# Sums, products and scalings of an attention kernel moved to GpSimd, its fillers left out, and its order given as tables

## The chip, the cores and the metric

One core of a Trainium2 chip. The kernel is one program for five engines that run side by side and wait for each other through semaphores: TensorE (PE in the profile; PEld is its weight loading), VectorE (DVE), ScalarE (ACT), GpSimd (POOL) and SyncE (SP), which issues nearly all transfers. The metric is the device time of one execution in microseconds; the time before is the median of three runs.

## What is computed

Two attentions over the same input x (2048 rows, 512 columns, 32 heads of 16), mixed by a gate of each row.

```python
def _A_ref(x, wqkv, w_phi, wo):          # linear attention with softmax features
    q, k, v = ...                         # 32 heads of 16
    pq = jnp.einsum("bhsd,hdf->bhsf", q, w_phi)
    pk = jnp.einsum("bhsd,hdf->bhsf", k, w_phi)
    phi_q = jnp.concatenate([_softmax(pq), _softmax(-pq)], axis=-1)
    phi_k = jnp.concatenate([_softmax(pk), _softmax(-pk)], axis=-1)
    kv = jnp.einsum("bhsf,bhsd->bhfd", phi_k, v)
    z  = jnp.einsum("bhsf->bhf", phi_k)
    num = jnp.einsum("bhqf,bhfd->bhqd", phi_q, kv)
    den = jnp.einsum("bhqf,bhf->bhq", phi_q, z)[..., None] + 1e-6
    return (num / den) @ wo               # heads put side by side

def _B_ref(x, wqkv, wo):                 # ordinary softmax attention
    scores = jnp.einsum("bhqd,bhkd->bhqk", q, k) * (Dh ** -0.5)
    return jnp.einsum("bhqk,bhkd->bhqd", _softmax(scores), v) @ wo

g = sigmoid((x * gate_w).sum(-1, keepdims=True))
return g * _A_ref(x, ...) + (1 - g) * _B_ref(x, ...)
```

## The kernel before, in words

**B, the bulk.** Scores are made transposed, keys on partitions and 512 queries along the free axis. There are 2048 such tiles of 128 x 512: 32 blocks (a block is four heads in four row groups of TensorE, with one chunk of 512 queries), 16 key tiles, four heads. A tile's exponential is taken on one of two paths.

- *ScalarE's path*: `add_qk` (L1305) puts two tiles into two PSUM banks, `add_exp` (L1389) takes the exponential of both in one instruction of 128 x 1024 into the ring `Ebuf`, and `add_pv` (L1443) multiplies them with V into the accumulator `psO`. Two pairs of banks alternate, so the scores of pair j + 2 need the exponential of pair j. This makes 652 exponentials.
- *The path of VectorE and GpSimd* (`add_group`, L1360): 744 tiles in groups of up to four. VectorE writes the score, offset and cut at zero, as a 16-bit integer whose bits are read as bf16: an approximate power of two (L1378; L1368 where two neighbouring banks go in one instruction). GpSimd adds a constant to these bits, four 16-bit words at a time, with `int64_add` (`shifted`, L1354), once to get a second term and, after TensorE has used that, once more for a third. `add_pvd` (L1416) multiplies the first two terms with V, and then the third (L1413). Each group holds two buffers from the lists in `PHASES`, which rotate.

The denominator comes as a 17th column of V. `add_norm` (L1504) drains a finished block (L1507), takes the inverse sums through small transfers and a reciprocal (L1516), and VectorE multiplies the result by them (L1523).

**A, beside it.** `phi` (L1658) projects 128 rows at a time onto the features, ScalarE takes both exponentials, and TensorE sums the 16 features of each head with 16 accumulating matmuls against the identity (L1676), two row tiles in one bank. For keys VectorE takes the reciprocal (L1691) and scales V with it (L1650). For queries VectorE takes a reciprocal, a copy and a product (L1682, L1684, L1686), and `scaled_q` (L1699) scales the negative features by the ratio (L1703); transfers then turn the features (`q_write`, `q_turn`). `kfinal` (L1731) masks the product of key features and V (L1732, L1735). `v_pair` (L1165) projects V for two head rows at once, with full 128-column matmuls of 256 (L1166).

**Order.** All work is recorded as operations with an engine, a planned duration, a priority and dependencies. `Plan.layout` (L538) plays the plan through with these durations and so fixes each engine's order and the PSUM banks. It also puts *fillers* on TensorE, matmuls with a zero operand (`zero_mm`, L1401), where its planned activity of the last microseconds falls under a limit. `Plan.settle` (L780) then applies the lists in `MOVES`: instructions of one engine that change places, pairs of VectorE tiles that are joined, banks, and fillers that are dropped. An operation marked `lock` is not planned while the other of VectorE and GpSimd runs one. Each engine runs its list strictly in that order; `emit` (L825) puts a semaphore wait ahead of an instruction where a dependency needs it, and whatever stands behind a waiting instruction on its engine waits too.

Of the kernel before, what the change touches and what calls it, by code (L numbers as in the profile page):

```python
# [9 lines left out]
F32 = mybir.dt.float32  # L10
# [21 lines left out]
PHASES = ((0, ("x0", "x1", "pq", "o3", "y0"), ("y1", "pt", "woA", "woB", "o2")),  # L32
          (16, ("x0", "x1", "n0", "a0", "y0", "wk"), ("y1", "a1", "a2", "a3", "wv")),
          (27, ("x0", "x1", "n0", "a0", "y0", "wk"), ("y1", "a1", "a2", "a3", "wv", "wq")))
SIZES = (2, 2)
STICK = 58.273
# [39 lines left out]
ERING = 2 * EPAIRS  # L76
LAT, BANK_LAT = 0.12, 0.12
# [3 lines left out]
MOVES = {  # L81
# [9 lines left out]
    ),  # L91
    "act": (
# [3 lines left out]
    ),  # L96
# [383 lines left out]
class Plan:  # L480
# [48 lines left out]
    def choose(self, op, banks):  # L529
# [4 lines left out]
        if op.half is not None:  # L534
            self.filled.setdefault(op.half[0], {})[op.half[1]] = (best.index, op.half[1])
# [1402 lines left out]
```

## Time and profile before

| | us |
|---|---|
| runs: median (lowest, highest) | 676.08 (675.73, 676.28) |
| profiled execution, its span | 673.9 |
| TensorE busy | 665.2 (99%) |
| ScalarE busy | 643.0 (95%) |
| VectorE busy | 602.8 (89%) |
| GpSimd busy | 401.0 (59%) |

The profile is of one execution; its span runs from the first to the last recorded instruction. In the lists of groups, a row gives the line, the engine, the operation, output <- input, the shapes and the count, then the busy time of all of them in microseconds and the mean of one in nanoseconds, then the idle time of the engine just before them and what ended most of it. Matmuls overlap each other, so a busy TensorE can still be mostly waiting; the waits tell. In the list of waits, a row gives the waiting engine, tile and line, what it waited for, the total in microseconds, the number of waits and the longest. The row PEclk gives the TensorE clock that was granted, in tenths of the full one, in 40 slices of the span.

### The profile page before, as it was taken

The page shows a single profiled execution, that of the slowest core. Times are in us where ns is not written, and L with a number is a line of the kernel's source. Part 1 is how long each engine was busy: PE and PEld are TensorE (multiplying, and loading weights), DVE is VectorE, ACT ScalarE, POOL GpSimd, SP SyncE. Part 2 cuts the span into 40 slices and gives each one's busy share as a digit, 9 for nine tenths or more (in the row PEclk, how much of TensorE's full clock was granted, in tenths as well). Part 3 has the DMA queues.
Part 4 walks back from the last instruction along what each step waited for, and adds up shares of the span by engine and source line. Part 5 has one row for each costly group of instructions (what it writes and reads, how often), then busy time and mean ns, then how long its engine had stood idle before and what let it go on. Part 6 is the DMA issues. An engine that isn't in the chain of part 4 may idle for free.

```text
span 673.9 us, 20931 instructions
## 1 busy us (share of the span) xinstructions
PE 665.2 (99%) x8995; PEld 233.7 (35%) x8995; DVE 602.8 (89%) x952; ACT 643.0 (95%) x723; POOL 401.0 (59%) x432
## 2 busy tenths in 40 slices
PE   8999999999999999999999999999999999999997
PEld 4332333434333333333333233323333233333333
DVE  4699889999998889999898989899999989999985
ACT  6999999999999999999999999999989998899995
POOL 7055557465666446565577676666865666555862
PEclk9999999999999999999999999999999999999999
DMA  7810101001010000000013032222311224032231
GB/s 129 157 40 12 32 13 26 11 11 23 7 27 11 11 21 8 19 17 15 21 41 102 26 67 62 54 44 64 77 54 41 63 77 105 18 89 66 66 72 40
DMA packets 67468, 30.95 MB, mean 46 GB/s; under 512 B 52696, under 2 KB 62296, under 8 KB 67376
## 3 DMA queue, kind: packets, MB, share of 16 engines
q1 hardware_dynamic: 66368, 28.95, 18.2%
q8 instruction: 70, 1.15, 0.7%
q10 hardware_dynamic: 576, 0.52, 0.2%
q0 software_dynamic: 432, 0.15, 0.2%
q14 instruction: 22, 0.18, 0.1%
HBM read 7.87 MB, written 8.88 MB: 25 GB/s over the span
## 4 chain that ended last, share of the span: by engine, by line
PE 81%; DVE 9%; ACT 7%; DMA 1%; issue 1%; SPq 0%; DVEq 0%
PE psS L1301 29%; PE psO L1413 28%; PE psS L1062 14%; ACT E_t L1392 6%; PE psS L1676 3%; DVE Tx_t L1378 2%; PE psO L1403 2%; DVE Ty_t L1378 1%; PE psS L1153 1%; PE psS L1166 1%; DVE WAT_t L1378 1%; DMA ld<-Tf_t 1%; PE psS L1773 1%; DMA Lq_t<-ld 1%; DVE vA_t L1378 1%
## 5 line engine op out<-in xcount | busy, mean ns | idle before, releaser
L1392 ACT ACTIVATE E_t<-psS 128x1024 bf16<-128x1024 f32 x652 | 611.6, 1049 | 20.0 <-PE psS L1301 16.1
L1301 PE MATMUL psS<-qz_t,kTB_t 32*128 32x512 bf16 x2048 | 272.9, 384 | 3.0 <-ACT E_t L1392 0.8
L1378 DVE TENSOR_SCALAR Tx_t<-psS 128x512 int16<-128x512 f32 x250 | 164.3, 681 | 13.2 <-PE psS L1301 11.8
L1301 PEld LDWEIGHTS psS<-qz_t,kTB_t 32*128 32x128 bf16 x2048 | 72.8, 91 | 231.5 <-ACT E_t L1392 100.7
L1413 PE MATMUL psO<-E_t,vaug_t 128*32 128x512 bf16 (+1 forms) x1304 | 106.4, 383 | 0.1
L1354 POOL INT64_ADD vA_t<-vA_t x72 | 71.5, 1001 | 35.7 <-PE psO L1413 21.3
L1378 DVE TENSOR_SCALAR Ty_t<-psS 128x512 int16<-128x512 f32 x110 | 73.7, 681 | 6.1 <-PE psS L1301 5.5
L1354 POOL INT64_ADD Ty_t<-Ty_t x42 | 43.3, 1032 | 15.0 <-PE psO L1413 10.2
L1413 PE MATMUL psO<-vA_t,vaug_t 128*32 128x512 bf16 (+1 forms) x520 | 49.9, 383 | 0.0
L1378 DVE TENSOR_SCALAR Tz_t<-psS 128x512 int16<-128x512 f32 x62 | 42.0, 685 | 3.3 <-PE psS L1301 2.2
L1413 PE MATMUL psO<-Ty_t,vaug_t 128*32 128x512 bf16 x436 | 43.9, 383 | 0.0
L1378 DVE TENSOR_SCALAR WAT_t<-psS 128x512 int16<-128x512 f32 x58 | 39.2, 685 | 4.2 <-PE psS L1301 3.8
L1354 POOL INT64_ADD phiQT_t<-Tx_t x19 | 18.1, 950 | 40.8 <-DVE Tx_t L1378 37.7
L1378 DVE TENSOR_SCALAR oT_t<-psS 128x512 int16<-128x512 f32 x56 | 37.4, 683 | 5.1 <-PE psS L1301 4.8
L1354 POOL INT64_ADD Ty_t<-Tx_t x29 | 29.7, 1025 | 20.4 <-DVE Tx_t L1378 12.1
L1413 PEld LDWEIGHTS psO<-E_t,vaug_t 128*32 128x32 bf16 (+1 forms) x1304 | 27.4, 95 | 35.3 <-issue 22.5
L1062 PE MATMUL psS<-Wp_t,xT_t 128*32 128x512 bf16 x512 | 37.7, 382 | 0.0
L1378 DVE TENSOR_SCALAR vA_t<-psS 128x512 int16<-128x512 f32 x52 | 35.1, 683 | 2.4 <-PE psS L1301 1.9
L1062 PE MATMUL psS<-xT_t,WB_t 128*32 128x512 bf16 x464 | 36.6, 383 | 0.0
L1354 POOL INT64_ADD vA_t<-Tx_t x22 | 22.0, 1002 | 21.5 <-DVE Tx_t L1378 17.5
L1378 DVE TENSOR_SCALAR Wp_t<-psS 128x512 int16<-128x512 f32 x48 | 31.9, 682 | 2.6 <-PE psS L1301 2.3
L1413 PE MATMUL psO<-Tx_t,vaug_t 128*32 128x512 bf16 x282 | 29.7, 387 | 0.0
(166 smaller groups left out, 914.4 us busy)
## 6 DMA issues: line engine op xcount, KB each, us to landing
dpq<-EA_t SPq DMA_DIRECT2D x16, 256.0 KB, 2.1
Rb_t<-lr SPq DMA_DIRECT2D x120, 32.0 KB, 1.8
dpo<-kv_t SPq DMA_DIRECT2D x16, 128.0 KB, 1.8
qz_t<-qz_t SPq DMA_DIRECT2D x120, 16.0 KB, 1.8
Tf_t<-Tf_t SPq DMA_DIRECT2D x60, 32.0 KB, 2.0
WB_t<-in_B_wqkv_dram SPq DMA_DIRECT2D x3, 384.0 KB, 4.3
out_dram<-WvA_t SPq DMA_DIRECT2D x8, 128.0 KB, 1.9
out_dram<-WB_t SPq DMA_DIRECT2D x6, 128.0 KB, 1.8
```

What stands on the lines that cost most here:

```text
L1062: ins = e.matmul(out[32 * i:32 * i + 32, :], lhsT=lhsT[:, 32 * i:32 * i + 32], rhs=rhs, start=start, stop=stop, tile_position=(0, 32 * i))
L1153: mms = [lambda e, ap, i=i, t=t: e.matmul(ap[:, 128 * i:128 * (i + 1)], lhsT=xT[:, t, NQ * c + 128 * i:NQ * c + 128 * (i + 1)], rhs=W_B[:, ...
L1166: mms = [lambda e, ap, i=i, t=t: e.matmul(ap[:, 256 * i:256 * (i + 1)], lhsT=xT[:, t, NQ * c + 128 * (2 * hf + i):NQ * c + 128 * (2 * hf + ...
L1301: return e.matmul(bank, lhsT=kT_B[32 * i:32 * i + 32, ROW[b // 2] % 2, 128 * kt:128 * (kt + 1)], rhs=qz[32 * i:32 * i + 32, b // 2 % 4, b ...
L1354: op = P.add("pool", P64 + W64 * size, d_prio(g["ts"][0]) - 5.0 + (0.0 if key == "s" else M_LATE), lambda e: e.int64_add(words(dst), words ...
L1378: ops.append(drain(f, mm, "dve", 0.70, d_prio(d), lambda e, ap, q=q: e.tensor_scalar(quarter(tb, q).bitcast(I16), ap, EXPB, 0.0, op0=ALU.a ...
L1392: op = P.add("act", EXP_OVH + 0.4267 * n, 0.0, lambda e: e.activation(Ebuf[:, j // 2 % EPAIRS, 512 * SZ[0] * (j % 2):512 * SZ[0] * (j % 2) ...
L1403: ins = e.matmul((psO if bank is None else bank)[32 * i:32 * i + 32, :], lhsT=zero[:], rhs=xT[:, 0, 0:NQ], start=bank is not None, stop=ba ...
L1413: return e.matmul(psO[32 * i:32 * i + w, :], lhsT=vaug[:, kt, o:o + w], rhs=rhs, start=start, stop=stop, tile_position=(0, 32 * i), skip_g ...
L1676: mms = [lambda e, ap, n=n, f=f: e.matmul(ap[:, 64 * n:64 * n + 64].rearrange("p (s g j) -> p s g j", s=2, j=4), lhsT=ident[:], rhs=es[n][ ...
L1773: mms = [lambda e, ap, g=g: e.matmul(ap[:, 64 * g:64 * g + 64], lhsT=qT(g)[:, 128 * j:128 * (j + 1)], rhs=kzbd[:, g, 0:64], start=True, st ...
```

## The change

- The feature sums of A leave TensorE: GpSimd adds halves four times, 16 features to 8, 4, 2 and 1, as 128 TensorTensor instructions, into the buffers `half` (which lies over the weights `Wbd` and `Wbp`, after their use) and `quart`.
- The product with the inverse sums (15 of them), the ratio of query features (8), the scaling of the negative query features (16) and the two masks of `kfinal` go from VectorE to GpSimd. The copy of the sums is no longer needed. The reciprocals stay on VectorE and read SBUF.
- `v_pair` uses `columns`: four matmuls of 32 columns in place of one of 128.
- No filler is left on TensorE. `layout` and `settle` go; `place` reads each engine's whole order, the banks and the joined pairs from `TABLE`. No operation is locked against another by the plan.
- The buffer `Tz` goes. From the third block on, both halves of `WAT` serve as buffers.
- `WIDE`, a way to give one exponential three tiles, is there but empty.

GpSimd's `int64_add` and its TensorTensor come from different libraries of operations. The build puts an instruction that reloads the library ahead of an operation that the loaded one does not have; copies, casts and fills are in every one. An excerpt of the changed program's order on GpSimd, the number of the instruction ahead (an ISA without operands is a reload; an ISA with tiles is a 64-bit add; L1365 are the sums, L1200 the products):

```
60 L1365 ISA
61 L1365 TensorTensor stat_t<-Wbs_t 128x8x2x4
62 L1029 ISA
63 L1029 ISA WoB_t<-WAT_t 128x1024
...
120 L1365 ISA
121 L1365 TensorTensor Wbs_t<-phiK_t 128x512
122 L1029 ISA
123 L1029 ISA WoB_t<-Ty_t 128x1024
124 L1365 ISA
125 L1365 TensorTensor quart_t<-Wbs_t 128x256
126 L1029 ISA
127 L1029 ISA oT_t<-Tx_t 128x512
```

The diff, cut to its core:

```diff
-PHASES = ((0, ("x0", "x1", "pq", "o3", "y0"), ("y1", "pt", "woA", "woB", "o2")),
+PHASES = ((0, ("x0", "x1", "o3", "y0"), ("y1", "pt", "woA", "woB", "o2")),
+          (2, ("x0", "x1", "n0", "o3", "n1", "y0"), ("y1", "pt", "woA", "woB", "o2")),
...
-MOVES = {
+TABLE = {
...
+    def place(self, table):
+        self.closed = {b: list(b.last) for b in self.every}
+        for b in self.every:
+            b.first = b.free
+        homes = {7 if b.index is None else b.index: b for b in self.every}
+        known, bank = list(self.ops), iter(table["homes"])
+        for k, n in table["extra"]:
+            known[k].extra = n
+        self.order = {e: [known[k] if k >= 0 else self.filler(k) for k in table[e]] for e in ENGINES}
+        for op in self.order["pe"]:
+            if op.acq is not None:
+                op.acq.bank = homes[int(next(bank))]
...
-    Wbd = sb([128, KT, 128], name="Wbd")
-    Wbp = sb([128, KT, 128], name="Wbp")
+    Wbs = sb([128, 2, KT, 128], name="Wbs")
+    Wbd, Wbp = Wbs[:, 0], Wbs[:, 1]
+    half = Wbs[:].rearrange("p a t c -> p (a t c)").bitcast(F32)
...
+    quart = sb([128, 256], F32, name="quart")
...
-        mms = [lambda e, ap, i=i, t=t: e.matmul(
-            ap[:, 256 * i:256 * (i + 1)], lhsT=xT[...],
-            rhs=W_B[:, t, 2 * D + 256:3 * D], start=(t == 0), stop=(t == KT - 1)) for i in range(2) for t in range(KT)]
+        mms = [lambda e, ap, i=i, t=t: columns(
+            e, ap[:, 256 * i:256 * (i + 1)], xT[...],
+            W_B[:, t, 2 * D + 256:3 * D], t == 0, t == KT - 1) for i in range(2) for t in range(KT)]
...
-                P.add("dve", 0.7, -40, lambda e: e.tensor_tensor(oT[:, r, qc, :], Tf[:, 0, :], Rb[:], ALU.mult),
-                      reads=[("Tf", 0), "Rb"], writes=[("oT", qc, r)], name=f"T2.{b}").lock = True
+                P.add("pool", 1.25, -40, lambda e: e.tensor_tensor(oT[:, r, qc, :], Tf[:, 0, :], Rb[:], ALU.mult),
+                      reads=[("Tf", 0), "Rb"], writes=[("oT", qc, r)], name=f"T2.{b}")
...
-        mms = [lambda e, ap, n=n, f=f: e.matmul(ap[:, 64 * n:64 * n + 64]..., lhsT=ident[:],
-                                                rhs=es[n][0]...[:, f],
-                                                start=(f == 0), stop=(f == DH - 1)) for n in range(2) for f in range(DH)]
-        f, mm = fill(S_PRIO + prio, mms, [k for _, k in es] + ["ident"], name=f"S{qk}.{st}", chunk=8, dur=0.042, cols=64)
+        for n, (e_ap, ek) in enumerate(es):
+            src, k = e_ap.rearrange("p (h f j) -> p h f j", f=DH, j=4), DH
+            while k > 1:
+                k //= 2
+                if k > 1:
+                    to = (quart if k == 4 else half)[:, 0:64 * k].rearrange("p (h f j) -> p h f j", f=k, j=4)
+                    u, v = src[:, :, 0:k, :], src[:, :, k:2 * k, :]
+                else:
+                    to = pair[:, n, :].rearrange("p (s g j) -> p g s j", s=2, j=4)
+                    u, v = [src[:, :, x, :].rearrange("p (g s) j -> p g s j", s=2) for x in (0, 1)]
+                P.add("pool", 0.1 + 0.14 * k, prio, lambda e, to=to, u=u, v=v: e.tensor_tensor(to, u, v, ALU.add), ...)
+                src = to
...
-            drain(f, mm, "dve", 0.25, prio, lambda e, ap: e.tensor_copy(statq[...], three(ap)[:, :, 0, :]), ...)
-            P.add("dve", 0.25, prio, lambda e: e.tensor_tensor(ratio[:], ratio[:], statq[...], ALU.mult), ...).lock = True
+            P.add("pool", 0.25, prio, lambda e: e.tensor_tensor(ratio[:], ratio[:], pair[:, :, 0:32], ALU.mult), ...)
...
-        P.add("dve", 0.7, prio, lambda e: e.tensor_tensor(minus, minus, by, ALU.mult), ...).lock = True
+        P.add("pool", 1.25, prio, lambda e: e.tensor_tensor(minus, minus, by, ALU.mult), ...)
...
-        P.add("dve", 2.3, prio, lambda e: e.tensor_tensor(kzbd[:, :, 0:64], kv_sb[:, :, 0:64], mask64[...], ALU.mult), ...).lock = True
+        P.add("pool", 1.3, prio, lambda e: e.tensor_tensor(kzbd[:, :, 0:64], kv_sb[:, :, 0:64], mask64[...], ALU.mult), ...)
...
-    P.layout()
...
-    P.settle(MOVES)
+    P.place(TABLE)
```

More of the change, by code (lines that the diff above doesn't have):

```diff
@@ L35 @@
 SIZES = (2, 2)
+WIDE, WIDE_SPAN = (), (8, 540)
 STICK = 58.273
@@ L76 @@
 ERING = 2 * EPAIRS
+E_AT = [sum(1024 + 512 * (k in WIDE) for k in range(r)) for r in range(ERING + 1)]
 LAT, BANK_LAT = 0.12, 0.12
@@ L523, in join_writes @@
         self.readers[key] = []
-    def mates(self, a, b):
-        return PAIRING and b.kind == "D1" and a.half[0] == b.half[0] and abs(a.rel.bank.index - b.rel.bank.index) == 1 and (
-            a.half[1] - b.half[1]) * (a.rel.bank.index - b.rel.bank.index) > 0
-    def choose(self, op, banks):
-        def key(b):
-            cross = op.half is not None and any((b.index - k) * (op.half[1] - q) < 0 for k, q in self.filled.get(op.half[0], {}).values())
-            return cross, max([0.0] + [x.end for x in b.last])
-        best = min(banks, key=key)
-        if op.half is not None:
-            self.filled.setdefault(op.half[0], {})[op.half[1]] = (best.index, op.half[1])
-        return best
@@ L768, in join, with filler @@
+    def filler(self, kind):
+        op = Op("pe", 0.215, 0.0, None, "idle")
+        op.deps, op.kind = list(self.ground), "zero"
+        if kind == -3:
+            op.acq = op.rel = Fill(self.misc)
+            op.fn = lambda e: self.idle(e, op.acq.bank.ap)
+        else:
+            op.fn = self.idle if kind == -1 else self.idle_o
+        self.ops.append(op)
+        return op
     def join(self, op, other):
@@ L770, in join @@
         b, b2 = op.rel.bank.index, other.rel.bank.index
-        assert other.half[0] == n_g and abs(b - b2) == 1 and (q - q2) * (b - b2) > 0
+        assert other.half[0] == n_g and (q - q2) * (b - b2) > 0
         op.fn = lambda e, a=(min(q, q2), max(q, q2)), b=(min(b, b2), max(b, b2)): wide(e, a, b)
@@ L777, in join @@
         other.rel, other.twin = None, op
-        self.order["dve"].remove(other)
-    def settle(self, moves):
-        homes = {b.index: b for b in self.every}
-        for k, b in moves.get("banks", ()):
-            op = self.order["pe"][k]
-            op.acq.bank, op.banks = homes[b], [homes[b]]
-        q = list(self.order["dve"])
-        for a, k in moves.get("pairs", ()):
-            self.join(q[a], q[k])
-        for a, k in moves.get("locks", ()):
-            self.order["pool"][a].deps.append(q[k])
-        gone = set(moves.get("drop", ()))
-        self.order["pe"] = [o for k, o in enumerate(self.order["pe"]) if k not in gone]
-        for e in ENGINES:
-            q, pairs = self.order[e], moves.get(e, ())
-            left = {a for a, _ in pairs}
-            new = [o for k, o in enumerate(q) if k not in left]
-            for a, k in pairs:
-                new.insert(k, q[a])
-            self.order[e] = new
+    def place(self, table):
[10 more added lines that the diff above has]
+                op.acq.bank = homes[int(next(bank))]
+            op.banks = op.take if op.take is not None else [op.acq.bank] if op.acq is not None else []
+        for a, k in table["pairs"]:
+            self.join(known[a], known[k])
         for op in self.ops:
@@ L1006, in _build @@
                   name="wob", lat=5.0)]
-    warm = P.add("dve", 0.3, -10, lambda e: e.memset(Ebuf[:, 0, 0:512], 0.0), writes=[("E", 0)], name="wz")
+    warm = P.add("dve", 0.3, -10, lambda e: e.memset(Ebuf[:, 0:512], 0.0), writes=[("E", 0)], name="wz")
     def warm_fn(e):
@@ L1229, in _build @@
     cur, rot = 0, 0
+    is_wide = lambda j: j % ERING in WIDE and WIDE_SPAN[0] <= j < WIDE_SPAN[1]
     def next_tile():
@@ L1245, in _build @@
         j = len(slots)
-        act = [t for t in (next_tile() for _ in range(SZ[j % 2])) if t is not None]
+        act = [t for t in (next_tile() for _ in range(SZ[j % 2] + is_wide(j))) if t is not None]
         if not act:
@@ L1271, in _build @@
     bufs["wq"] = (Wp[:, :, 0:D], p_ops[0])
-    for k in range(1):
+    for k in range(2):
         bufs[f"n{k}"] = (flat(WAT[:, 4 * k:4 * k + 4, :]), wp_ops)
@@ L1315, in fn @@
             ins = None
-            for m, t in enumerate(ts):
+            for m, t in enumerate(ts[:2]):
                 ins = qk_mm(e, t, psS[:, 512 * (base + m):512 * (base + m + 1)])
@@ L1320, in add_qk @@
         op.full = 0.21
-        op.kind, op.heads = "qk", [t[1] for t in ts]
+        op.kind, op.heads = "qk", [t[1] for t in ts[:2]]
+        if len(ts) == 3:
+            third[j] = fill(-99, [lambda e, ap: qk_mm(e, ts[2], ap)], reads, [bS[lowS]], name=f"q3.{j}", after=exp_ops[j - 2:j - 1])
+            third[j][1].kind, third[j][1].heads = "q3", [ts[2][1]]
         op.lat += QK_PAD
@@ L1329, in add_qk @@
         return op
-    made, dq_ops, last_d1 = [0], [], []
+    made, dq_ops, last_d1, third = [0], [], [], {}
     holder = {}
@@ L1392, in add_exp @@
         op = P.add("act", EXP_OVH + 0.4267 * n, 0.0, lambda e: e.activation(
-            Ebuf[:, j // 2 % EPAIRS, 512 * SZ[0] * (j % 2):512 * SZ[0] * (j % 2) + 512 * n], psS[:, 512 * base:512 * (base + n)], ACTF.Exp, scale=ESCALE),
-            reads=[("S", j % 2)], writes=[("E", j % ERING)], name=f"exp{j}")
+            Ebuf[:, E_AT[j % ERING]:E_AT[j % ERING] + 512 * n], psS[:, 512 * base:512 * (base + n)], ACTF.Exp, scale=ESCALE),
+            reads=[("S", j % 2)], writes=[("E", j % ERING)], after=[third[j][1]] if j in third else [], name=f"exp{j}")
+        if j in third:
+            op.rel = third[j][0]
         op.kind, op.extra = "exp", j % 2
@@ L1453, in add_pv @@
                 pv_started.add((b, t[1]))
-                o = 512 * SZ[0] * (j % 2) + 512 * m
-                work.append((seen[t[1]], t, Ebuf[:, j // 2 % EPAIRS, o:o + 512], start))
+                o = E_AT[j % ERING] + 512 * m
+                work.append((seen[t[1]], t, Ebuf[:, o:o + 512], start))
                 seen[t[1]] += 1
@@ L1480, in add_pv @@
                        writes=["psO"] if first else (),
-                       after=pv_last[-1:] + (block_pvd.get(b, []) if last else []), name=f"pv{j}")
+                       after=pv_last[-1:] + (block_pvd.get(b, []) if last else []), name=f"pv{j}.{b}")
             op.full = 0.215 * rounds
@@ L1630, in gate @@
         P.add("dve", 0.2, 140, lambda e: e.reciprocal(omg, gT[:, 1, :]), reads=["g1"], writes=["omg"], name="g2")
-    xe = []
+    xe, wp_mms = [], []
     def wp_fill(qk, t, prio):
@@ L1638, in wp_fill @@
                      dur=0.07, cols=128)
+        wp_mms.append(mm)
         wp_ops.append(drain(f, mm, "dve", 0.69, prio, lambda e, ap: e.tensor_copy(Wp[:, t, D * qk:D * (qk + 1)], ap),
@@ L1679, in phi @@
-        f, mm = fill(S_PRIO + prio, mms, [k for _, k in es] + ["ident"], name=f"S{qk}.{st}", chunk=8, dur=0.042, cols=64)
-        if qk == 0:
-            three = lambda ap: ap[:, 0:128].rearrange("p (b s c) -> p b s c", b=2, s=2)
-            drain(f, mm, "dve", 0.55, prio, lambda e, ap: e.reciprocal(ratio[:], three(ap)[:, :, 1, :]), writes=["ratio"],
-                  name=f"rs{qk}.{st}", last=False)
-            drain(f, mm, "dve", 0.25, prio, lambda e, ap: e.tensor_copy(statq[:, st % 8 - 1:st % 8 + 1, 0:32], three(ap)[:, :, 0, :]),
-                  writes=[("sq", st % 8 - 1), ("sq", st % 8)], name=f"rp{qk}.{st}")
-            P.add("dve", 0.25, prio, lambda e: e.tensor_tensor(ratio[:], ratio[:], statq[:, st % 8 - 1:st % 8 + 1, 0:32], ALU.mult),
-                  reads=["ratio", ("sq", st % 8 - 1), ("sq", st % 8)], writes=["ratio"], name=f"rt{qk}.{st}").lock = True
+        pair = stat[:] if qk else statq[:, st % 8 - 1:st % 8 + 1, :]
@@ new lines, in phi @@
+        pkey = [("rs", 0), ("rs", 1)] if qk else [("sq", st % 8 - 1), ("sq", st % 8)]
+        for n, (e_ap, ek) in enumerate(es):
[5 more added lines that the diff above has]
+                    u, v = src[:, :, 0:k, :], src[:, :, k:2 * k, :]
+                else:
+                    to = pair[:, n, :].rearrange("p (s g j) -> p g s j", s=2, j=4)
+                    u, v = [src[:, :, x, :].rearrange("p (g s) j -> p g s j", s=2) for x in (0, 1)]
+                P.add("pool", 0.1 + 0.14 * k, prio, lambda e, to=to, u=u, v=v: e.tensor_tensor(to, u, v, ALU.add), reads=[ek if k == 8 else "quart" if k == 2 else "half"],
+                      writes=["half" if k in (8, 2) else "quart"] if k > 1 else [pkey[n]], after=wp_mms if k == 8 else (), name=f"h{qk}.{st - 1 + n}.{k}")
+                src = to
@@ L1688, in phi @@
+        if qk == 0:
+            P.add("dve", 0.55, prio, lambda e: e.reciprocal(ratio[:], pair[:, :, 32:64]), reads=[("sq", st % 8 - 1), ("sq", st % 8)],
+                  writes=["ratio"], name=f"rs{qk}.{st}")
+            P.add("pool", 0.25, prio, lambda e: e.tensor_tensor(ratio[:], ratio[:], pair[:, :, 0:32], ALU.mult),
+                  reads=["ratio", ("sq", st % 8 - 1), ("sq", st % 8)], writes=["ratio"], name=f"rt{qk}.{st}")
             for i in (st - 1, st):
@@ L1690, in phi @@
             return
-        drain(f, mm, "dve", 0.96, prio, lambda e, ap: e.reciprocal(stat[:], ap[:, 0:128].rearrange("p (b c) -> p b c", b=2)),
-              writes=[("rs", 0), ("rs", 1)], name=f"rs{qk}.{st}")
-        after = [mm]
+        P.add("dve", 0.96, prio, lambda e: e.reciprocal(stat[:], stat[:]), reads=[("rs", 0), ("rs", 1)], writes=[("rs", 0), ("rs", 1)],
+              name=f"rs{qk}.{st}")
         for i in (st - 1, st):
-            va_fill(i, prio, after)
+            va_fill(i, prio, [mm])
     pw_ops = []
@@ L1702, in scaled_q @@
         by = ratio[:, b, :].rearrange("p (g j) -> p g j", j=4).unsqueeze(2).to_broadcast([128, 8, DH, 4])
-        P.add("dve", 0.7, prio, lambda e: e.tensor_tensor(minus, minus, by, ALU.mult),
-              reads=["ratio", ("EA", b)], writes=[("EA", b)], name=f"phi0.{st}.1").lock = True
+        P.add("pool", 1.25, prio, lambda e: e.tensor_tensor(minus, minus, by, ALU.mult),
+              reads=["ratio", ("EA", b)], writes=[("EA", b)], name=f"phi0.{st}.1")
         q_write(st)
@@ L1731, in kfinal @@
     def kfinal(prio):
-        P.add("dve", 2.3, prio, lambda e: e.tensor_tensor(
+        P.add("pool", 1.3, prio, lambda e: e.tensor_tensor(
             kzbd[:, :, 0:64], kv_sb[:, :, 0:64], mask64[:].unsqueeze(1).to_broadcast([128, 8, 64]), ALU.mult),
-            reads=[("kv", 0), ("kv", 1), "mask64"], writes=["kz0"], name="kz0").lock = True
-        P.add("dve", 0.1, prio, lambda e: e.tensor_tensor(
+            reads=[("kv", 0), ("kv", 1), "mask64"], writes=["kz0"], name="kz0")
+        P.add("pool", 0.2, prio, lambda e: e.tensor_tensor(
             kzbd[:, :, 64:68], kv_sb[:, :, 64:68],
             mask4[:].unsqueeze(1).to_broadcast([128, 8, 4]), ALU.mult),
-            reads=[("kv", 0), ("kv", 1), "mask4"], writes=["kz1"], name="kz1").lock = True
+            reads=[("kv", 0), ("kv", 1), "mask4"], writes=["kz1"], name="kz1")
     def q_write(i):
@@ L1882, in _build @@
         if op in wo_ops:
-            op.deps = op.deps + phase_ops[0]
+            op.deps = op.deps + phase_ops[0] + phase_ops[1]
         if op.name.startswith("Tq0."):
-            op.deps = op.deps + phase_ops[0]
+            op.deps = op.deps + phase_ops[0] + phase_ops[1]
         if op.name.startswith("T2.") and int(op.name[3:]) >= 16:
-            op.deps = op.deps + phase_ops[0]
+            op.deps = op.deps + phase_ops[0] + phase_ops[1]
     for op in P.ops:
@@ L1899, in _build @@
     P.add("sp", 0.1, 1e6, lambda e: None, reads=[("out", i) for i in range(NT)], name="end")
-    P.layout()
-    q = P.order["pe"]
-    P.order["pe"] = [o for o, nxt in zip(q, q[1:] + [None]) if not (
-        o.name == "idle" and o.acq is None and nxt is not None and nxt.kind == "qk" and len(nxt.heads) == 3)]
-    P.settle(MOVES)
+    P.place(TABLE)
     sems = {e: sem("s_" + e) for e in ENGINES}
```

262 lines of the change are left out of this document (17 added, 245 removed), and 568 rows, old and new, of tables (MOVES, TABLE).

## The prediction

> **What bounds the kernel now.** I read the first part of the page, then the grouped waits, then the groups by line, then the timeline of GpSimd around its first 64-bit add.
>
> ```profile
> span 673.9 us, 20931 instructions
> PE 665.2 (99%) x8995; PEld 233.7 (35%) x8995; DVE 602.8 (89%) x952; ACT 643.0 (95%) x723; POOL 401.0 (59%) x432
> PEclk9999999999999999999999999999999999999999
> ```
> ```profile
> PEld psS L1301 <- ACT E_t L1392: 100.7, 256, 0.7
> ACT E_t L1392 <- PE psS L1301: 16.1, 42, 1.1
> ACT E_t L1392 <- PE psO L1413: 2.4, 2, 1.9
> ```
> ```profile
> L1392 ACT ACTIVATE E_t<-psS 128x1024 bf16<-128x1024 f32 x652 | 611.6, 1049 | 20.0 <-PE psS L1301 16.1
> L1378 DVE TENSOR_SCALAR Tx_t<-psS 128x512 int16<-128x512 f32 x250 | 164.3, 681 | 13.2 <-PE psS L1301 11.8
> L1368 DVE TENSOR_SCALAR Tx_t<-psS 128x1024 int16<-128x1024 f32 x16 | 19.5, 1218 | 2.0 <-PE psS L1301 1.8
> ```
>
> TensorE looks full at 99%, but its weight loads for the next scores wait 100.7 us for an exponential to free its banks. ScalarE is the engine that hardly waits: its exponentials hold 611.6 us and wait for TensorE 16.1 + 2.4 = 18.5 us in all. The 652 exponentials are the same in both kernels. So whatever the change takes off TensorE or VectorE, it can win at most these 18.5 us: no better than 676.1 - 18.5 = 657.6 us. A loss has no such bound. GpSimd has 673.9 - 401.0 = 272.9 us free, and the change spends there.
>
> **The change part by part: what is taken away.**
>
> ```profile
> L1403 PE MATMUL psO<-xT_t,zero_t 128*32 128x512 bf16 x264 | 25.6, 385 | 0.3 <-DVE Tf_t L1507 0.2
> L1403 PE MATMUL psS<-xT_t,zero_t 128*32 128x512 bf16 x36 | 3.4, 385 | 0.0
> L1676 PE MATMUL psS<-EA_t,ident_t 128*128 128x64 bf16 x256 | 9.8, 192 | 0.0
> L1676 PE MATMUL psS<-phiK_t,ident_t 128*128 128x64 bf16 x256 | 9.8, 192 | 0.0
> L1166 PE MATMUL psS<-WB_t,xT_t 128*128 128x256 bf16 x64 | 9.2, 275 | 0.0
> L1062 PE MATMUL psS<-WvA_t,xT_t 128*32 128x512 bf16 x256 | 19.6, 382 | 0.0
> L1523 DVE TENSOR_TENSOR oT_t<-Tf_t,Rb_t 128x512 bf16<-128x512 f32 x15 | 10.2, 682 | 0.0
> L1703 DVE TENSOR_TENSOR EA_t<-EA_t,ratio_t 128x512 bf16<-128x512 bf16 x16 | 10.8, 682 | 0.0
> L1686 DVE TENSOR_TENSOR ratio_t<-ratio_t,statq_t 128x64 f32<-128x64 f32 x8 | 1.7, 209 | 0.0
> L1684 DVE COPY statq_t<-psS 128x64 f32<-128x64 f32 x8 | 1.3, 168 | 0.0
> L1732 DVE TENSOR_TENSOR kzbd_t<-kv_t,mask_t 128x512 bf16<-128x512 f32 x1 | 0.7, 686 | 0.0
> ```
>
> In these rows stand line, engine, operation, tiles, shapes, count, then busy time and ns of one, then idle time before. TensorE loses the fillers (25.6 + 3.4 us) and the 512 sums over the identity (9.8 + 9.8 us). V of two head rows goes from 64 wide matmuls of 9.2 us to 256 of 32 columns each; the column-tiled row L1062 takes 19.6 us for 256 of twice the length, so 9.8 us: no change. Fillers stand where TensorE would wait anyway, so much of their 29 us becomes idle time. The rest goes first into the 100.7 us in which TensorE waits for ScalarE. VectorE loses 10.2 + 10.8 + 1.7 + 1.3 + 0.7 = 24.7 us, and gets 21 x 0.144 = 3 back: by the two programs' orders 33 pairs of score tiles are drained by one instruction instead of 54, and each parted pair costs 2 x 0.681 - 1.218 = 0.144 us. The reciprocals stay on VectorE and read SBUF instead of PSUM; the buffer Tz goes and WAT's two halves come in from the third block on, so that six tiles rotate instead of five; the new order on every engine keeps each engine's count of work. I cost these three at nothing: ScalarE's 611.6 us cover them, and what they could lose is inside rival D. All this counts for 0 to 18.5 us.
>
> **What is added on GpSimd.** 169 TensorTensor instructions: 64 of 512 elements (32 first sums, 15 products of attention, 16 scalings, 1 mask), 32 each of 256 and 128, 40 of 64, and one smaller. No two-input elementwise row of GpSimd exists; the nearest have one input.
>
> ```profile
> L1050 POOL COPY Wbp_t<-Wbd_t 128x512 bf16<-128x512 bf16 x1 | 1.1, 1081 | 3.5 <-DMA Wbd_t<-in_A_w_phi_dram 3.5
> L1655 POOL CAST vA_t<-stat_t 128x64 bf16<-128x64 f32 x16 | 3.7, 241 | 5.6 <-DVE stat_t L1691 5.1 <-DVE gT_t L1624 0.5
> ```
>
> The two rows give (1.081 - 0.241)/448 = 1.875 ns an element over 0.12 us. Below: 64 x 1.08 + 32 x 0.60 + 32 x 0.36 + 40 x 0.24 = 109 us. Above, with twice the time an element for two inputs, 199 us. I take 125, near the row of the same engine and size. GpSimd would then be busy 526 us of 674: room enough by itself.
>
> **The switches.** In the changed program's order on GpSimd, an instruction without operands, a reload of the library that GpSimd's operations come from, stands at every place where the stream passes from 64-bit adds to a TensorTensor or back. There are 217; the kernel before has one, ahead of its first 64-bit add, because its other GpSimd work (copies, casts, fills) needs none. So 216 are new. Between two visits to the TensorTensors stand 390/108 = 3.6 adds on average, and more than half of these stretches hold one or two. What one costs, the trace hardly tells:
>
> ```profile
> 16.97 1.08 POOL L1050 COPY Wbp_t<-Wbd_t 128x512 bf16<-128x512 bf16 x1 [3.52 <-DMA Wbd_t<-in_A_w_phi_dram]
> 31.83 1.89 DVE L1378 TENSOR_SCALAR Tx_t<-psS 128x512 int16<-128x512 f32 x3
> 33.23 0.61 POOL L1354 INT64_ADD phiQT_t<-Tx_t  x1 [15.18 <-DVE Tx_t L1378]
> 664.82 1.04 POOL L1354 INT64_ADD WB_t<-WB_t  x1 [0.40 <-PE psO L1413]
> ```
>
> The one switch lies in the 15.18 us between the copy and the add, which waited for VectorE's tiles. So a switch costs between nothing and 15 us. Where is it in that? [...]
>
> ```profile
> L1047 POOL DMA_DIRECT2D Wbd_t<-in_A_w_phi_dram x8 | 4.1, 520 | 0.2 <-POOL mask_t L1054 0.2
> L1794 ACT ACT_TABLE_LOAD x1 | 1.3, 1283 | 1.7 <-PEq L1923 1.7
> WoB_t<-in_B_wo_dram SPq DMA_DIRECT2D x1, 512.0 KB, 5.1
> Wbd_t<-in_A_w_phi_dram POOLq DMA_DIRECT2D x8, 2.0 KB, 2.6
> WB_t<-in_B_wqkv_dram POOLq DMA_DIRECT2D x1, 128.0 KB, 4.5
> ```
>
> [...] GpSimd can hide (272.9 - 125)/216 = 0.68 us a switch at best, if they were spread evenly; beyond that it is the bound. [...]
>
> What a late switch holds up: the 64-bit adds queued behind it on GpSimd; the value products on TensorE (L1413) that read those tiles; behind these in TensorE's order the next scores; so the next exponential on ScalarE. The products of attention and the feature scalings are late too, and the transfers behind them on SP's queue.
>
> **The sum**, on GpSimd, the new bound. The row is the busy time of the 64-bit adds alone, over the whole span:
>
> ```profile
> 0.00:674.00 674.00, 384.63 (x390) 1.00 0.19 46
> ```
>
> Start until the copy's end 18.1; 390 adds 384.6; casts 3.7; TensorTensor 125; switches 216 x 5.6 = 1,210; waits that stay, the first 15.2 and half of what the 111 adds in runs of ten or more without a switch wait now (272.9/390 = 0.70 us each), 39; after the last add's end at 665.9, 8.0. Together 1,804 us. The span lies 2.2 us under the runs' median of 676.08 us, so the forecast is about 1,805 us.
>
> **Rivals.**
> (A) The switch is nearly free (both libraries stay in place). For it: no fetch of code stands in the trace near 18 us. Against it: the wait there would cover 15 us of anything. Then GpSimd fits at 526 us, and ScalarE gets most of its 18.5 us back: about 663 us, faster. It decides below about 0.3 us a switch, half of the 0.68 that an even spread would hide.
> (B) It is as dear as ScalarE's table load, 1.28 us: 216 x 1.28 = 276 us instead of 1,210, so about 870 us. For it: the nearest row of a unit that changes its functions. [...] I let it stand for 0.6 to 3 us, 725 to 1,240 us.
> (C) It takes most of the 15 us: at 15.0 the sum is 3,830 us, at 11 about 2,970. [...]
> (D) Free switches, but the chains of four sums (about 2.3 us) stand in front of adds that TensorE waits for. 32 chains late by 1.2 us are 38 us, less some of the gain: about 700 us. Against: GpSimd waits 272.9 us now, so an add is seldom the last thing to come.
>
> **Chances.** Forecast (3 to 8 us a switch, 1,240 to 2,320 us) 0.62; B 0.13; C 0.10; A 0.11; D 0.04. The range leaves out A, D, the cheapest of B and C beyond 9.7 us a switch, 0.2 together: 820 to 2,700 us. Faster by over 0.2%, which is about what a measurement of this kernel can tell, is A: 0.10; within it 0.02 from A and D; slower 0.88.
>
> **What the profile would show.** If I am right: GpSimd has a gap of some 5 to 6 us before most TensorTensor rows and before the add after them, put down to nothing that computes; ScalarE's busy time stays near 643 us but falls to some 36% of the span; TensorE's weight loads wait for GpSimd's adds, where now they wait for ScalarE; TensorE's granted clock no longer shows 9 throughout. If TensorTensor rows of 512 elements show 1.1 to 1.3 us, that part is right. If the gaps are under 0.3 us and ScalarE is above 95%, the price of the switch was wrong and A holds; if the gaps are long but follow VectorE or DMA, the cause is another.

## The result and the profile after

The changed kernel takes 2054.1 us (median; 2053.1 to 2055.0), three times as long: the ratio to the kernel before, run beside it at 675.9 us, is 3.036 [3.031, 3.041]. The profiled execution has a span of 2051.4 us. Here and below a median is of all runs of a kernel, while a ratio and its 95% interval leave out runs over 1.5% above the fastest of the same kernel. The first part of its page, with the share of the span behind each busy time:

```profile
span 2051.4 us, 20276 instructions
PE 852.7 (42%) x8375; PEld 220.7 (11%) x8375; DVE 597.3 (29%) x922; ACT 668.8 (33%) x723; POOL 523.6 (26%) x601
PEclk9866656775655656656556556566555556556578
issue 56%; PE 20%; POOL 15%; ACT 5%; DVE 3%; DMA 1%; SPq 0%; POOLq 0%; DVEq 0%
```

No engine is busy for half of the span; before, TensorE was at 99% and ScalarE at 95%. The fourth row is the chain of work that ended last: 56% of it is "issue", time in which an engine waited for nothing that the profile records. GpSimd, the new bound, is busy 26%. So what holds it is not work. The grouped waits say who suffers:

```profile
ACT E_t L1067 <- PE psS L973: 1316.8, 277, 39.1
PEld psO L1090 <- POOL vA_t L1029: 354.6, 33, 39.2
DVE Tx_t L1053 <- PE psS L973: 270.7, 76, 27.2
```

ScalarE's exponentials waited 16.1 us for TensorE's scores and now wait 1,316.8 us. TensorE's weight loads waited for ScalarE and now wait for GpSimd's 64-bit adds. Where GpSimd's own time goes stands in its timeline (start, duration, row, and in brackets the idle time just before):

```profile
70.52 1.04 POOL L1029 INT64_ADD WoB_t<-WoB_t  x1 [1.79 <-PE psO L1090]
78.67 1.27 POOL L1200 TENSOR_TENSOR oT_t<-Tf_t,Rb_t 128x512 bf16<-128x512 f32 x1 [7.11 <-issue]
85.78 1.03 POOL L1029 INT64_ADD Ty_t<-Ty_t  x1 [5.84 <-issue]
86.80 1.03 POOL L1029 INT64_ADD WoA_t<-Tx_t  x1
...
115.87 0.31 POOL L1365 TENSOR_TENSOR stat_t<-Wbs_t 128x64 f32<-128x64 f32 x1 [7.15 <-issue]
121.92 1.03 POOL L1029 INT64_ADD WoB_t<-WAT_t  x1 [5.75 <-issue]
```

Each passage from an add to a TensorTensor leaves about 7.1 us without a row, each passage back about 5.8 us, and instructions of one kind follow each other at once. For one product of 1.27 us the adds stand still from 71.56 to 85.78 us. Added up over all rows of this timeline, the 108 idle times ahead of a TensorTensor behind a switch are 775.4 us (median 7.14, 6.72 to 7.79) and the 108 ahead of the add after it 642.4 us (median 5.94, the shortest 5.65): 1,417.8 us for 216 switches, 6.56 us each. The groups of the TensorTensors carry the first sum nearly whole, as the idle time behind the bar; five of them:

```profile
L1365 POOL TENSOR_TENSOR Wbs_t<-quart_t 128x128 f32<-128x128 f32 x32 | 14.2, 445 | 129.0 <-issue 128.0
L1365 POOL TENSOR_TENSOR quart_t<-Wbs_t 128x256 f32<-128x256 f32 x32 | 23.2, 726 | 116.0 <-issue 114.8
L1365 POOL TENSOR_TENSOR Wbs_t<-phiK_t 128x512 f32<-128x512 bf16 x16 | 18.4, 1147 | 73.9 <-ACT E_t L1067 29.3 <-issue 29.1 <-ACT phiK_t L1346 14.8
L1200 POOL TENSOR_TENSOR oT_t<-Tf_t,Rb_t 128x512 bf16<-128x512 f32 x15 | 18.8, 1254 | 85.5 <-issue 85.5
L1387 POOL TENSOR_TENSOR EA_t<-EA_t,ratio_t 128x512 bf16<-128x512 bf16 x16 | 16.6, 1049 | 58.2 <-issue 58.0
```
```profile
0.00:2051.40 2051.40, 384.19 (x390) 0.63 0.06 15
```

The sums of 128 elements take 14.2 us and stand behind 129.0 us of idle time. The trace also holds two records of 0.01 us for each reload, which these views leave out (434 in this kernel, 2 in the kernel before). The first of the two begins 0.03 us (median) after the instruction ahead of it ends, so the idle time starts with the reload. The last row, from the view of stretches, is the busy time of the adds alone over the whole span, 384.19 us as before, with the mean granted clock of TensorE, 0.63, behind the count. So GpSimd's 2,051.4 us are 523.6 of work, 1,417.8 of switches and 110.0 of all other idle time.

### The profile page after: what moved, and what is told of

It is laid out like the page before. It is cut to its first block, busy times and chain, and to the rows that moved or that the text cites. A ratio compares the mean times of both kernels' runs of the same rounds, so it can differ in the third digit from the quotient of the medians.

```text
span 2051.4 us, 20276 instructions
## 1 busy us (share of the span) xinstructions
PE 852.7 (42%) x8375; PEld 220.7 (11%) x8375; DVE 597.3 (29%) x922; ACT 668.8 (33%) x723; POOL 523.6 (26%) x601
## 4 chain that ended last, share of the span: by engine, by line
issue 56%; PE 20%; POOL 15%; ACT 5%; DVE 3%; DMA 1%; SPq 0%; POOLq 0%; DVEq 0%
PE psO L1090 9%; PE psS L973 7%; ACT E_t L1067 4%; PE psS L732 4%; POOL vA_t L1029 3%; POOL Wbs_t L1365 2%; POOL Ty_t L1029 2%; POOL quart_t L1365 1%; POOL WB_t L1029 1%; POOL WoB_t L1029 1%; POOL oT_t L1029 1%; POOL oT_t L1200 1%; POOL EA_t L1387 1%; POOL phiQT_t L1029 1%; POOL WoA_t L1029 1%
## 5 line engine op out<-in xcount | busy, mean ns | idle before, releaser
L1067 ACT ACTIVATE E_t<-psS 128x1024 bf16<-128x1024 f32 x652 | 635.9, 1050 | 1341.8 <-PE psS L973 1316.8
L973 PE MATMUL psS<-qz_t,kTB_t 32*128 32x512 bf16 x2048 | 346.1, 480 | 59.5 <-DVE Tx_t L1053 20.2
L1090 PE MATMUL psO<-vA_t,vaug_t 128*32 128x512 bf16 (+1 forms) x520 | 69.4, 516 | 275.5 <-POOL vA_t L1029 228.9
L1053 DVE TENSOR_SCALAR WAT_t<-psS 128x512 int16<-128x512 f32 x154 | 103.8, 685 | 260.1 <-PE psS L973 259.4
L1090 PE MATMUL psO<-E_t,vaug_t 128*32 128x512 bf16 (+1 forms) x1304 | 135.0, 479 | 35.9 <-DVE Tf_t L1184 35.8
L1090 PE MATMUL psO<-Ty_t,vaug_t 128*32 128x512 bf16 (+1 forms) x428 | 57.6, 520 | 173.8 <-POOL Ty_t L1029 108.4
L1090 PE MATMUL psO<-oT_t,vaug_t 128*32 128x512 bf16 x196 | 26.5, 510 | 167.2 <-POOL oT_t L1029 111.1
L1090 PE MATMUL psO<-WAT_t,vaug_t 128*32 128x512 bf16 x176 | 23.3, 501 | 78.7 <-POOL Ty_t L1029 25.7
L1365 POOL TENSOR_TENSOR quart_t<-Wbs_t 128x256 f32<-128x256 f32 x32 | 23.2, 726 | 116.0 <-issue 114.8
L1365 POOL TENSOR_TENSOR Wbs_t<-EA_t 128x512 f32<-128x512 bf16 x16 | 18.3, 1143 | 115.8 <-ACT E_t L1067 59.1
```

The costliest lines, as they stand in the source:

```text
L973: return e.matmul(bank, lhsT=kT_B[32 * i:32 * i + 32, ROW[b // 2] % 2, 128 * kt:128 * (kt + 1)], rhs=qz[32 * i:32 * i + 32, b // 2 % 4, b ...
L1053: ops.append(drain(f, mm, "dve", 0.70, d_prio(d), lambda e, ap, q=q: e.tensor_scalar(quarter(tb, q).bitcast(I16), ap, EXPB, 0.0, op0=ALU.a ...
L1067: op = P.add("act", EXP_OVH + 0.4267 * n, 0.0, lambda e: e.activation(Ebuf[:, E_AT[j % ERING]:E_AT[j % ERING] + 512 * n], psS[:, 512 * bas ...
L1090: return e.matmul(psO[32 * i:32 * i + w, :], lhsT=vaug[:, kt, o:o + w], rhs=rhs, start=start, stop=stop, tile_position=(0, 32 * i), skip_g ...
L1365: P.add("pool", 0.1 + 0.14 * k, prio, lambda e, to=to, u=u, v=v: e.tensor_tensor(to, u, v, ALU.add), reads=[ek if k == 8 else "quart" if k ...
```

## The experiments

Three explanations are on trial. Theory 1: the switches, some 6.56 us each, make the loss. Rival 1: the missing fillers let TensorE's clock fall (0.63), and that makes it. Rival 2: the work moved to GpSimd makes it.

**The change without its switches** (`e1_copies`).

```diff
-lambda e, to=to, u=u, v=v: e.tensor_tensor(to, u, v, ALU.add)
+lambda e, to=to, u=u: e.tensor_copy(to, u)
...
-e.tensor_tensor(oT[:, r, qc, :], Tf[:, 0, :], Rb[:], ALU.mult)
+e.tensor_copy(oT[:, r, qc, :], Tf[:, 0, :])
```

> The changed kernel with each of its 169 TensorTensors on GpSimd replaced by a copy or cast of one operand, of the same shape where there is one, so that nothing needs a library other than the adds' own. It leaves out the feature sums, the products with the inverse sums and the ratio, the scaling and the masks; everything else of the change stays (no fillers, V in column tiles, the tables). Theory 1 (the 216 switches make the loss, about 6.56 us each): without them the time is 655 to 690 us, the reloads but for one are gone from the trace, and the granted clock is back near 1. Rival 1 (TensorE without fillers runs at a low clock, and that sets the time): the fillers are still missing, so the time stays above 900 us and the clock near 0.63. Rival 2 (the work added to GpSimd sets the time): the copies keep about 100 of the 124 us, so the time stays far above 700 us.

Measured: 660.9 us (660.4 to 662.1), ratio to before 0.977 [0.976, 0.979]. Its page and ScalarE's wait for scores:

```profile
span 658.9 us, 19844 instructions
PE 645.4 (98%) x8375; PEld 211.1 (32%) x8375; DVE 583.3 (89%) x922; ACT 637.6 (97%) x723; POOL 466.3 (71%) x601
PEclk9999999999999999999999999999999999999999
```
```profile
ACT E_t L1067 <- PE psS L973: 8.5, 22, 0.7
```

With the same order, the same column tiles and no filler, but nothing that needs another library, 1,393 us are gone and the clock is full. The trace holds the records of one reload alone. Rival 1 falls here: without the switches' waits the same TensorE without fillers keeps its clock (granted 1.00, against 0.63 in the changed kernel), so the low clock of the changed kernel follows from those waits, which hold TensorE's weight loads for up to 39.2 us at a time. How the clock follows from their length was not shown. What is left of rival 2 is the difference between TensorTensors and copies on GpSimd, 523.6 - 466.3 = 57 us; the copies take 66 us, less than the 100 that had been expected.

**The switches without the change** (`e2_dose`).

```diff
+    dead = sb([128, 64], name="dead")
+    adds = [o for o in P.order["pool"] if o.name.startswith("s64.")]
+    for n, o in enumerate(adds[10::10]):
+        d = P.add("pool", 0.2, 0, lambda e, n=n: e.tensor_tensor(dead[:, 2 * n:2 * n + 2], zero[:, 0:2], zero[:, 0:2], ALU.add), ...)
+        P.order["pool"].insert(P.order["pool"].index(o), d)
```

> The kernel before, plus 19 TensorTensors of two elements on data that nothing reads, one ahead of every tenth first add of GpSimd's list: 38 switches, next to no work. Theory 1: each visit costs GpSimd 7.14 + 5.94 = 13.1 us, 19 visits 249 us, less what GpSimd's 273 us of idle time hides around them; as the adds behind a visit are late at once, I expect most of it to show, 800 to 925 us, with the two gaps at 7.1 and 5.9 us. A switch of nothing, or one that can be hidden: 674 to 690 us. Rivals 1 and 2: the fillers are there and the work is 2 us, so 674 to 680 us.

Measured: 923.8 us (916.3 to 926.4) against 676.3, ratio 1.362 [1.358, 1.366]: 247.5 us more, at the upper end of what was expected. Its page, the group of the added instructions, that of the exponentials, and one visit in the timeline:

```profile
span 924.6 us, 21026 instructions
PE 723.6 (78%) x8995; PEld 238.5 (26%) x8995; DVE 608.0 (66%) x952; ACT 651.1 (70%) x723; POOL 403.8 (44%) x451
PEclk9997959897988798898798868797979788798869
```
```profile
L1909 POOL TENSOR_TENSOR dead_t<-zero_t 128x2 bf16<-128x2 bf16 x19 | 3.5, 183 | 135.5 <-issue 121.0 <-DVE Tf_t L1507 7.5 <-DVE Ty_t L1378 7.0
L1392 ACT ACTIVATE E_t<-psS 128x1024 bf16<-128x1024 f32 x652 | 619.3, 1042 | 260.7 <-PE psS L1301 256.2
```
```profile
62.88 1.04 POOL L1354 INT64_ADD phiQT_t<-Tx_t  x1 [3.26 <-DVE Tx_t L1378]
70.97 0.18 POOL L1909 TENSOR_TENSOR dead_t<-zero_t 128x2 bf16<-128x2 bf16 x1 [7.06 <-issue]
76.94 1.03 POOL L1354 INT64_ADD WoB_t<-oT_t  x1 [5.78 <-issue]
```

19 instructions that work 3.5 us in all cost 135.5 us ahead of them, 7.13 each, and (summed from the timeline) 112.9 us behind them, 5.94 each: 248.4 us, and the time grew by 247.5. ScalarE's wait for scores grew from 16.1 to 256.2 us. The switch alone makes this loss, with all fillers in place, and the clock falls with it, to 0.86.

**The same work in fewer visits** (`e5_grouped`). An excerpt of GpSimd's new order, the number of the instruction ahead; the product and the eight sums of two row tiles now share one visit:

```
46 L1199 ISA
47 L1199 TensorTensor oT_t<-Tf_t,Rb_t 128x512
48 L1364 TensorTensor Wbs_t<-phiK_t 128x512
...
55 L1364 TensorTensor stat_t<-Wbs_t 128x8x2x4
56 L1028 ISA
57 L1028 ISA Ty_t<-Ty_t 128x1024
```

> The changed kernel with another order on GpSimd alone: neighbouring TensorTensors with up to six 64-bit adds between them are put side by side, where no dependency forbids it. Every operation of the change is kept; GpSimd goes to the TensorTensors 23 times instead of 108, so 46 switches instead of 216. Theory 1: 661 us (the changed kernel without any switch) plus 23 visits at 13.1 us, 301 us, is 962 us; some 10 to 50 us more if the sums, now late for the adds behind them, hold those up: 930 to 1,020 us. Rival 2 (the TensorTensors themselves are the load, 124 us of them, all kept): the time stays near 2,054 us.

Measured: 1,059.8 us (1,054.6 to 1,061.9), ratio 1.566 [1.562, 1.570]. All the work is there and 994 us are gone with 170 switches, so rival 2 falls. The time lies 40 us above the range that was expected. The first lines of its page, and VectorE's wait for sums:

```profile
span 1051.5 us, 19933 instructions
PE 729.3 (69%) x8375; PEld 215.8 (21%) x8375; DVE 589.4 (56%) x922; ACT 651.8 (62%) x723; POOL 524.9 (50%) x601
```
```profile
DVE ratio_t L1368 <- POOL statq_t L1364: 96.6, 7, 15.7
```

The 46 switches are 298.5 us in the timeline, as expected. The expectation started from the kernel with copies and forgot that the TensorTensors take 524.9 - 466.3 = 58.6 us longer; the rest between the two spans, 1,051.5 - 658.9 - 298.5 - 58.6 = 35.5 us, is idle time of GpSimd. Among what is late are the sums: VectorE stands up to 15.7 us before a reciprocal of them, with the score tiles queued behind it.

The spans of four kernels, split on GpSimd (us):

| kernel | switches | busy | at new switches | other idle | span |
|---|---|---|---|---|---|
| before | 1 | 401.0 | 0 | 272.9 | 673.9 |
| before, 19 visits | 39 | 403.8 | 248.4 | 272.4 | 924.6 |
| changed, grouped | 47 | 524.9 | 298.5 | 228.1 | 1,051.5 |
| changed | 217 | 523.6 | 1,417.8 | 110.0 | 2,051.4 |

A new switch costs 6.54, 6.49 and 6.56 us in the three.

**The fillers** (`e3_nofill`).

```diff
+        self.order["pe"] = [o for o in self.order["pe"] if o.name != "idle"]
+        for op in self.ops:
+            op.extra = 0 if op.kind == "pv" else op.extra
```

> The kernel before without its 300 fillers on TensorE (their 25.6 + 3.4 us become idle time); nothing else is changed. Theory 1: the clock does not need them, since TensorE is then still busy for some 95% of the span; 670 to 680 us, granted clock above 0.97. Rival 1: the clock falls well below 0.95 and the time rises above 750 us.

Measured: 685.2 us, scattered from 676.4 to 690.6, ratio 1.009 [1.006, 1.012], which is 6 us; more than theory 1 had allowed, and nothing like rival 1. The scatter goes with the granted clock: runs took 676.4 us at 0.997, the time of the kernel before, 682.7 at 0.987 and 685.5 at 0.978. The profiled run took 685.0 us at 0.980. In stretches of its span (busy time with count of PE, PEld, DVE, ACT, POOL, then the clock):

```profile
0.00:17.00 17.00, 13.89 (x109) 6.62 (x109) 7.31 (x27) 10.17 (x12) 13.41 (x26) 0.85 0.65 132
17.00:34.00 17.00, 17.00 (x124) 5.60 (x123) 4.22 (x7) 12.11 (x12) 0.00 (x0) 0.55 0.75 150
34.00:68.00 34.00, 32.22 (x347) 10.09 (x351) 33.00 (x50) 33.91 (x38) 15.58 (x16) 1.00 0.07 21
68.00:683.00 615.00, 604.51 (x8123) 209.62 (x8115) 558.14 (x870) 588.32 (x663) 371.20 (x390) 0.99 0.17 41
```

and the second stretch of the kernel before, then its fillers in that stretch alone (PE, PEld, the clock):

```profile
17.00:34.00 17.00, 17.00 (x207) 5.92 (x205) 11.32 (x18) 17.00 (x20) 1.82 (x3) 1.00 0.83 158
17.00:34.00 17.00, 3.39 (x36) 0.85 (x36) 1.00 0.83 158
```

From 17 to 34 us the clock is 0.55 instead of 1.00, TensorE issues 124 matmuls instead of 207 - 36 = 171 that are not fillers, and ScalarE runs 12 instructions instead of 20. From 34 to 68 us the clock is 1.00 again, and from there to the end 0.99. In this run of this order the fillers' worth lies mostly in the start; in the order of the tables (`e1_copies`) the clock is full from the start without them.

**Column tiles for V** (`e4_vcols`).

```diff
-        mms = [lambda e, ap, i=i, t=t: e.matmul(
+        mms = [lambda e, ap, i=i, t=t: columns(
```

> The kernel before with only the V of two head rows in column tiles: 256 matmuls of 32 columns in place of 64 of 128. The prediction costs them at 9.8 us against 9.2 and so at nothing: 674 to 678 us. If a switch between the two tilings of TensorE costs something, each of the 8 calls shows it: 16 changes of tiling, and the time rises above 680 us.

Measured: 676.0 us, ratio 0.999 [0.998, 1.001]. Its group has the 256 small matmuls in 9.6 us:

```profile
L1062 PE MATMUL psS<-WB_t,xT_t 128*32 128x256 bf16 x256 | 9.6, 274 | 0.0
```

**Can the 15 us be had with all work done?** `c1_back` keeps the tables and takes every TensorTensor off GpSimd.

```diff
+        f, mm2 = fill(prio, mms, [k for _, k in es] + ["ident"], name=f"S{qk}.{st}", chunk=4 if qk else 5, dur=0.042, cols=64)
+            drain(f, mm2, "dve", 0.55, prio, lambda e, ap: e.reciprocal(ratio[:], three(ap)[:, :, 1, :]), ...)
...
-                P.add("pool", 1.25, -40, lambda e: e.tensor_tensor(oT[:, r, qc, :], Tf[:, 0, :], Rb[:], ALU.mult),
+                P.add("dve", 0.7, -40, lambda e: e.tensor_tensor(oT[:, r, qc, :], Tf[:, 0, :], Rb[:], ALU.mult),
```

> The changed kernel's tables, column tiles and missing fillers, but with no TensorTensor on GpSimd: the feature sums are again 16 accumulating matmuls against the identity, put by hand into one of the three rotating score banks right behind the second exponential, and the products, the ratio, the scalings and the masks are again on VectorE. All work is done. Theory 1: no switch is left, so the loss is gone; of the 15 us that the kernel with copies won, the 19.6 us of TensorE and 25 us of VectorE that come back take some: 660 to 690 us, faster than the kernel before only if the bank that each sum holds for some 2 us costs less than 1 us of ScalarE's time.

Measured: 729.2 us (718.7 to 737.3), ratio 1.072 [1.066, 1.077]. No: slower than before, and by more than expected.

```profile
PE 687.3 (94%) x8887; PEld 228.1 (31%) x8887; DVE 615.2 (85%) x971; ACT 647.2 (89%) x723; POOL 408.6 (56%) x432
```
```profile
ACT E_t L1065 <- PE psS L971: 63.1, 91, 3.1
```

ScalarE's wait for scores is 63.1 us instead of 8.5 in the kernel with copies. Two more kernels split this; each is the kernel with copies with one half of the work back.

```diff
 c3_prods, on the kernel with copies
-                P.add("pool", 1.25, -40, lambda e: e.tensor_copy(oT[:, r, qc, :], Tf[:, 0, :]),
+                P.add("dve", 0.7, -40, lambda e: e.tensor_tensor(oT[:, r, qc, :], Tf[:, 0, :], Rb[:], ALU.mult),
 c4_sums, on c1_back
-                P.add("dve", 0.7, -40, lambda e: e.tensor_tensor(oT[:, r, qc, :], Tf[:, 0, :], Rb[:], ALU.mult),
+                P.add("pool", 1.25, -40, lambda e: e.tensor_copy(oT[:, r, qc, :], Tf[:, 0, :]),
```

> The changed kernel without library switches, where only the products with the inverse sums, the ratio, the scalings and the masks are back on VectorE; the feature sums stay copies on GpSimd, so this leaves out the feature sums. It splits the 68 us between the kernel with copies (661 us) and the one with all work back on VectorE and TensorE (729 us). 41 instructions of 25 us come back to VectorE, whose busy time goes from 583 to about 608 of 659 us. If VectorE's load is what costs, 685 to 700 us; if the score bank that each sum on TensorE holds is what costs, this one stays at 661 to 672 us.

> The other half: only the feature sums are back, on TensorE against the identity, each pair of row tiles in one of the three rotating score banks; the products, the scalings and the masks stay copies on GpSimd, so this leaves out those products and masks. 16 sums, each of which takes 1.2 us of TensorE and holds a bank that the score tiles of VectorE rotate through. If the bank is what costs, 2 to 3 us each: 690 to 715 us; if VectorE's load is what costs, 661 to 675 us.

Measured: 692.9 us with the products on VectorE (689.4 to 701.7, ratio 1.023 [1.020, 1.026]) and 700.3 us with the sums on TensorE (698.7 to 702.8, 1.037 [1.034, 1.039]). Each had been expected to carry the loss alone. Taken from the ratios, they are 31 and 40 us over the kernel with copies (0.977), together 71 where both at once (1.072) cost 64: they nearly add up, and neither is free. The busy times of the two, in this order; the first page is of the run of 701.7 us:

```profile
PE 668.8 (96%) x8375; PEld 211.9 (30%) x8375; DVE 611.6 (87%) x963; ACT 645.0 (92%) x723; POOL 450.2 (64%) x560
```
```profile
PE 670.0 (96%) x8887; PEld 228.6 (33%) x8887; DVE 590.2 (85%) x938; ACT 641.2 (92%) x723; POOL 419.3 (60%) x465
```

In the first, 28 us more work on VectorE (583.3 to 611.6) cost 31 us, though VectorE has spare time on the average; in the second, 16 sums cost 2.5 us each. Part of this goes with the clock: runs of `c3_prods` took 689.4 us at a granted clock of 0.990 and 694.0 at 0.982, runs of `c1_back` 718.7 at 0.995 and 729.0 at 0.974. What starts it, VectorE's load in the one and the score banks in the other, was not shown: a sum's bank was not tested apart from TensorE's own 1.2 us and from the 7 us that VectorE gets back with the sums (583.3 to 590.2). These instructions were put into a finished order by hand; a new order around them, as the kernel before has, was not run. The kernel before stays the fastest that does all the work.

## Why the prediction was right, and where its numbers were off

- **What bounds the kernel, and the 18.5 us at most**: not contradicted. Without switches 15.5 us (676.3 to 660.9) came, under the bound of 18.5. But the bound took ScalarE's work as fixed, and only part of the gain is the wait: ScalarE's idle time fell by 9.6 us (30.9 to 21.3; its main wait went from 16.1 to 8.5), its busy time by 5.4 (643.0 to 637.6). Why the latter fell is open.
- **What is taken away**: the V tiles are worth nothing, as costed (9.6 us for 9.8). The parted pairs were miscounted: the rows after show 35 joined pairs, not 33, so VectorE gets 19 x 0.144 = 2.7 us back. That a filler left out only becomes idle time was wrong for the order before, by some 6 us that go with the clock, and had no part in the result: in the tables' order without switches the clock holds.
- **What is added on GpSimd**: 169 TensorTensors taken at 125 us; the rows of the profile add up to 123.4, and those of 512 elements have 1.05 to 1.25 us.
- **The switches**: the step that decided the sign, and it held: 216, hardly hidden, on the path. Mis-sized was the price: 5.6 us in the sum, 6.56 measured. This is 216 x 0.96 = 207 us of the 248 by which the sum of 1,804 fell short of the span. No run shows the term of 5.6 us: it was the author's estimate, one issue of GpSimd (0.52) and the slowest landing (5.1) in the prediction's rows, and no run shows that a switch is such a transfer; the two instruction queues on the pages (q8 and q14) move as many packets before (70 + 22) as after (65 + 27). In its place the runs showed 7.14 us for the switch to the TensorTensors and 5.94 us for the one back to the adds. That the estimate came so near is in part luck.
- **Remaining waits, start and tail**: 18.1 + 15.2 + 39 + 8.0 = 80 us in the sum; measured 2,051.4 - 384.2 - 3.6 - 123.4 - 1,417.8 = 122. This is the other 42 us. Start (15.5 for 18.1), first wait (16.3) and tail (9.9) are near their terms, so half of the free adds' waits, the 39 us, was too little.
- **That GpSimd's idle time might hide 0.68 us a switch**: in `e2_dose` none was hidden. GpSimd's idle time outside the switches stayed at 272.4 us of 272.9: the engines that its adds wait for stood still with it, as ScalarE's 256.2 us of waiting show. In the changed kernel 192.6 us (`e1_copies`: 658.9 - 466.3) shrank to 110.0, so 0.38 us a switch.
- **Rivals**: A (nearly free), B (1.28 us) and D (late sums alone) fall with the price of 6.5 us in three kernels, and D also with `e1_copies`, where the chains stand in the same places as copies; C (11 to 15 us) falls too: of the 15.18 us ahead of the first add before, a switch at the measured 5.94 us is less than half.
- **What the profile would show**: ScalarE's share 33% for 36%, TensorE's loads waiting for the adds, the clock down: as written. The gap was to be 5 to 6 us on both sides; ahead of the TensorTensors it is longer.

## What to carry to other kernels

Before work goes to GpSimd, look which library each operation there comes from: here a TensorTensor between two 64-bit adds cost 1.3 us of work and 13.1 us of silence, and an engine that idles 40% of the span hid none of it in the kernel before. If the two must mix, count visits, not instructions (108 to 23 visits took 994 us off); if they need not, copies and casts were free of it (`e1_copies`, with one reload, took 660.9 us). And a kernel whose engines feed each other in a ring has less room than its idle times say: 25 us of products put back on an engine with 76 us to spare cost 31.

## What the runs showed of the hardware that was not expected

- A switch's price depends on its direction: 7.14 us to the TensorTensors, 5.94 us back to the adds, the same in three kernels (7.13 and 5.91; 7.16 and 5.86). Why was not tried.
- A switch has no busy row of its own in the groups; beside the two short records of its reload it shows only as idle time under "issue", or under whatever else ended meanwhile (29.3 us of it "ACT E_t" above).
- In the order before, leaving out all 300 fillers cost nothing in the run that kept its clock (676.4 us at 0.997) and 9 us in one that lost 2% of it (685.5 at 0.978). In the profiled run the loss of clock lay almost only near the start: 0.55 instead of 1.00 from 17 to 34 us, 0.99 from 68 us to the end.
